# Attention products with the values on quarters of the TensorE array, attention in two PSUM rings, and a new order of the work

## The chip, the cores and the metric

The kernel runs on one core of a Trainium2 chip. The metric is the device time of one execution in microseconds (us); less is better. The engines are named as the profile names them: PE is TensorE (matmuls; PEld is its weight load), DVE is VectorE, ACT is ScalarE, POOL is GpSimd, SP is the engine that issues the DMAs. Each engine works through its own queue in the order in which the program lists it.

## What is computed

Attention with a window of 128 positions over 4 x 8 heads (576 positions, 64 wide), then a two-layer MLP over the 2304 tokens, then an expert layer for tokens with a positive skip score. The kernel counts the tokens with a positive score and leaves the expert layer out where there are none, as in the execution profiled here.

```python
scores = scale * np.matmul(q, k.transpose(0, 1, 3, 2))
mask = (rel >= 0) & (rel < window)                   # window = 128
scores = np.where(mask, scores + bias[None], -1000000000.0)
attn = np.exp(scores - scores.max(-1)); attn = attn / (attn.sum(-1) + 1e-09)
x = np.matmul(attn, v)                               # then (tokens, 512)
h = x @ w_in                                         # 512 -> 2048
g = where(h >= 1, h, where(h <= -1, 0, (h + 1) ** 2 / 4))
x = g @ w_out                                        # 2048 -> 512
```

## The kernel before

The 2304 tokens are nine blocks `g` of 256 queries (two tiles of 128). `pair` (L312) is the attention of one block for two heads; there are four pairs to a block, 36 in all. `tile_ff` (L516) is one step of the MLP: 256 tokens by two of the sixteen groups of 128 hidden units, so eight steps to a block, 72 in all. Weights and activations of the MLP are split into a high and a low float32r part, and each product is three matmuls: a step has 24 matmuls of 256 columns into `h` (L528, here "first product") and 12 of 512 columns into the block's two sums (L559, "second product", six for each tile of tokens). `weight` (L463) unpacks the weights, which come in as float64, in integer operations on DVE with copies on ACT; that work lies in about the first 120 us. Blocks 0 to 2 run interleaved, so that a weight is used three times while the next is unpacked; blocks 3 to 8 follow one after the other, with the attention of a later block between their steps.

A pair goes through these stages. SP loads q and k (`qkraw`) and v (`vraw`); q is scaled on ACT or POOL (L334, L336). PE makes the scores. For blocks 0 and 1 (`whole`) two heads lie in two row halves of the array, with 256 columns each (L347). From block 2 on, 64 queries by 192 keys at a time, so that four matmuls lie on the four 64 x 64 quarters of the array (L359). DVE puts the two parts of the window together under a mask (L370 or L376, "merge"), adds the bias and takes the row maximum (L382). ACT takes the exponential of each tile and head (L388), four to a pair. DVE inverts the sums (L397, L398). The rows are normalised on ACT (L416) or POOL (L419), transposed on PE (L424) into a PSUM bank, and copied to `pts` on ACT (L293). POOL masks the copy into `ab` (L307), four selects to a pair. PE multiplies with the values (L446): for each head one matmul of 256 columns and two of 128 columns, on a 128 x 64 half of the array, the two heads side by side. The result is copied to `xT` by ACT (L293) and its low part made by DVE (L302).

PSUM has eight banks, in four rings of two: `h` for the first product, and `r0`, `r1`, `r2`. For blocks 3 to 8 all attention goes through `r0`: scores (two banks), transposed rows (two) and products with the values (one), one after another. The sums of the second product alternate between `r2` and `r1`.

The order of the instructions on every engine is worked out before the kernel is built. `Plan.order` places the pieces with costs written in the source (for instance 2 * dve(128) + 0.06 us for the merge of one head, L391), keeps for each engine a list of what can run and takes what is due first; due times come from `PLAN` (`lead`, `spread`, `d2` and others). It is five passes over all pieces, and the tile pools then add the waits. Where the plan sees PE idle in the first 40 us, L603 puts in matmuls without use ("fills").

Of the kernel before, what the change touches and what calls it, by code (L numbers as in the profile page):

```python
# [11 lines left out]
F32 = mybir.dt.float32  # L12
# [6 lines left out]
ALU = mybir.AluOpType  # L19
# [3 lines left out]
P = 128  # L23
B, H, S, D = 4, 8, 576, 64
NT = B * S
DM = H * D
# [5 lines left out]
NPAIR = H // 2  # L32
# [13 lines left out]
PLAN = dict(base=4.418, d0=10.283, d1=3.632, d3=3, d2=5.432, lag=1, lag2=9, ahead=19.774, lead=22.491, spread=2,  # L46
            margin=1.2, slack=0.049, fin=0.449, passes=5, first=3, stick=4.711, zeros=0, whole=2)

ENGINES = dict(norm="AP", wlo="DP", rebias="A", pt="A", whi="A", square="A", scale="AP")
# [48 lines left out]
class Plan:  # L98
# [139 lines left out]
dve = lambda n: n / 960.0 + 0.072  # L238
# [7 lines left out]
class Fused:  # L246
# [50 lines left out]
    def pick(self, key, **cost):  # L297
        return {e: cost[e] for e in ENGINES[key]}

# [12 lines left out]
    def pair(self, g, p, due):  # L312
# [26 lines left out]
        lq = add(self.pick("scale", A=0.4, P=0.43, D=dve2(256)), scale, [lq], use=[qk], port=True)  # L339
        s = [self.att(g, [P, 2, 4, 64]) for _ in heads]  # L340
# [20 lines left out]
        sn = self.buf("sn", 2, [P, 4, P])  # L361
# [40 lines left out]
        for odd, o in heads:  # L402
            pt = self.bank("r1", [P, 2, P]) if g < 2 else self.att(g, [P, 2, P])
# [28 lines left out]
            d = add(self.pick("norm", A=0.586, D=dve(256), P=0.67), norm, [rs], use=[sn, st], port=True)  # L432
            d = self.chain("tr", add({"T": 0.221}, transpose, [d], new=[pt, pts], use=[sn]))
            d = add(self.pick("pt", A=actp(256), D=dve(256)), lambda e, ptv=ptv, pts=pts: self.copy(e, pts.t, ptv()), [d],
# [4 lines left out]
        av = self.att(g, [P, 2, P]) if g else self.bank("r0", [P, 2, P])  # L439

        def avs(e):
            for out, k, m, more in ((slice(0, 2), j, slice(1, 3), False), (0, 0, 0, True), (1, j + 1, 3, True)):
                if g == 0 and k == 0 and more:
                    continue
                for o, ab, _ in last:
                    nc.tensor.matmul(av.t[o, out, :], v.t[:, k, o], ab.t[:, m, :], start=not more, stop=True,  # L446
                                     skip_group_check=more)

        d = add({"T": 0.92 if g else 0.71}, avs, [lv, last[0][2], last[1][2]], new=[av], use=[v, last[0][1], last[1][1]],
                mode="cols")  # L450
        new = []
        if g not in self.xT:
# [4 lines left out]
        d1 = add({"A": actp(256)}, lambda e: self.copy(e, xT.t[:, 0, p], av.t), [d], new=new, use=[av, xT])  # L457
        d2 = add({"D": dve(256)}, lambda e: self.sub(e, xT.t[:, 1, p], av.t, xT.t[:, 0, p].bitcast(F32)), [d, d1],
                 use=[av, xT], due=due)
# [145 lines left out]
    def run(self):  # L605
# [231 lines left out]
```

## Time and profile before

| | |
|---|---|
| time, median of 3 runs | 527.0 us (526.81 to 528.45) |
| profiled execution, its own time | 527.1 us |
| its span in the profile | 525.3 us |
| PE busy | 509.4 us (97%) |
| PEld busy | 429.9 us (82%) |
| DVE busy | 277.2 us (53%) |
| ACT busy | 301.4 us (57%) |
| POOL busy | 100.7 us (19%) |
| granted TensorE clock, mean | 0.995 |

The 1.8 us between span and time lie outside what the profiler records. A matmul's busy time in the profile includes its latency, so that neighbours overlap; what a group of matmuls costs PE is read from the start of the group to the start of the next one.

### The profile page before, as it was taken

The page shows a single profiled execution, that of the slowest core. Times are in us where ns is not written, and L with a number is a line of the kernel's source. Part 1 is how long each engine was busy: PE and PEld are TensorE (multiplying, and loading weights), DVE is VectorE, ACT ScalarE, POOL GpSimd, SP SyncE. Part 2 cuts the span into 40 slices and gives each one's busy share as a digit, 9 for nine tenths or more (in the row PEclk, how much of TensorE's full clock was granted, in tenths as well). Part 3 has the DMA queues.
Part 4 walks back from the last instruction along what each step waited for, and adds up shares of the span by engine and source line. Part 5 has one row for each costly group of instructions (what it writes and reads, how often), then busy time and mean ns, then how long its engine had stood idle before and what let it go on. Part 6 is the DMA issues. An engine that isn't in the chain of part 4 may idle for free.

```text
span 525.3 us, 10059 instructions
## 1 busy us (share of the span) xinstructions
PE 509.4 (97%) x3700; PEld 429.9 (82%) x3702; DVE 277.2 (53%) x844; ACT 301.4 (57%) x784; POOL 100.7 (19%) x244
## 2 busy tenths in 40 slices
PE   7999999999999999999999999999999999999994
PEld 3567898888888898889888988888888988889883
DVE  5989999998365225532555236422653265223221
ACT  6999778777477336643575237633763277433330
POOL 2673000234014200330033002400231013200000
PEclk9999999999999999999999999999999999999997
DMA  8565555553121202120212012210212020101001
GB/s 268 163 231 192 189 178 151 190 172 113 49 90 52 61 1 92 50 61 1 67 52 65 21 49 67 57 32 1 91 52 60 1 92 1 31 0 41 1 0 44
DMA packets 27141, 41.12 MB, mean 78 GB/s; under 512 B 2000, under 2 KB 15952, under 8 KB 27088
## 3 DMA queue, kind: packets, MB, share of 16 engines
q1 hardware_dynamic: 26416, 40.12, 24.2%
q8 instruction: 30, 0.49, 0.4%
q10 hardware_dynamic: 672, 0.33, 0.2%
q14 instruction: 23, 0.19, 0.1%
HBM read 35.72 MB, written 4.72 MB: 77 GB/s over the span
## 4 chain that ended last, share of the span: by engine, by line
PE 76%; DVE 11%; ACT 5%; DMA 3%; issue 2%; POOL 0%; SPq 0%; ACTq 0%; POOLq 0%; DVEq 0%
PE h L528 32%; PE r L559 32%; PE r L446 6%; PE r L359 4%; ACT sn L388 2%; PE r L424 2%; DVE stage L494 2%; DVE wtmp L499 2%; DVE r L376 2%; DMA qkraw<-in_qk 1%; DMA stage<-in_w_in 1%; DMA stage<-in_w_out 1%; DVE stage L480 1%; DVE sn L382 1%; ACT sn L416 1%
## 5 line engine op out<-in xcount | busy, mean ns | idle before, releaser
L528 PE MATMUL h<-xT,wi 128*128 128x256 f32 x1728 | 222.9, 282 | 0.6 <-POOL wi L302 0.4
L528 PEld LDWEIGHTS h<-xT,wi 128*128 128x128 f32 x1728 | 213.6, 188 | 11.7 <-issue 5.2
L559 PE MATMUL r<-wo,g 128*128 128x512 f32 x864 | 219.1, 400 | 0.0
L559 PEld LDWEIGHTS r<-wo,g 128*128 128x128 f32 x864 | 156.0, 188 | 37.7 <-issue 4.4
L550 DVE SCALAR_TENSOR_TENSOR h<-h,u 128x512 f32<-128x512 f32 x72 | 50.3, 698 | 129.3 <-ACT u L545 126.6
L540 ACT ACTIVATE u<-h,half 128x512 f32<-128x512 f32 x72 | 49.4, 686 | 111.1 <-PE h L528 110.5
L419 POOL TENSOR_SCALAR sn<-sn,st 128x128 f32<-128x128 f32 x70 | 27.1, 400 | 237.4 <-ACT u L540 175.7
L388 ACT ACTIVATE sn<-sn,st 128x128 f32<-128x128 f32 x144 | 56.1, 391 | 27.1 <-DVE st L382 27.0
L307 POOL TENSOR_SCALAR_AFFINE_SELECT ab<-pts 128x256 f32<-128x256 f32 (+1 forms) x144 | 56.5, 426 | 53.5 <-ACT pts L293 44.0
L293 ACT ACTIVATE g<-h 128x512 fp32r<-128x512 f32 x72 | 42.8, 594 | 33.1 <-DVE h L550 32.9
L302 DVE TENSOR_TENSOR g<-h,g 128x512 fp32r<-128x512 f32 x72 | 49.6, 689 | 22.2 <-ACT g L293 21.3
L545 ACT ACTIVATE u<-u 128x512 f32<-128x512 f32 x72 | 45.5, 632 | 1.4
L376 DVE COPY_PREDICATED r<-mask,r 64x128 f32<-64x128 uint8 x112 | 33.2, 296 | 15.9 <-PE r L359 12.9
L446 PE MATMUL r<-ab,vraw 128*64 128x128 f32 (+1 forms) x416 | 35.6, 315 | 3.5 <-ACT pts L293 1.7
L446 PEld LDWEIGHTS r<-ab,vraw 128*64 128x64 f32 x416 | 25.2, 136 | 14.6 <-issue 3.8
L382 DVE CUSTOM_DVE_ANT_0 sn<-r,nrel 128x128 f32<-128x128 f32 x144 | 33.3, 286 | 0.8
L574 DVE CUSTOM_DVE_ANT_0 junk<-r,wskip 128x512 f32<-128x512 f32 x18 | 12.4, 691 | 37.1 <-ACT stage L293 36.5
L388 ACT ACTIVATION_READ_ACCUMULATOR sn<-sn,st 128x1 f32 x144 | 27.0, 188 | 0.0
L416 ACT ACTIVATE sn<-sn,st 128x128 f32<-128x128 f32 x74 | 25.4, 394 | 1.7 <-DVE st L398 1.2
L424 PE MATMUL r<-ident,sn 128*128 128x128 f32 x144 | 23.7, 277 | 1.6 <-POOL sn L419 1.2
L474 ACT ACTIVATE wtmp<-stage 128x512 f32<-128x512 f32 x32 | 21.7, 679 | 5.3 <-DVE wi L302 2.2
L359 PE MATMUL r<-qkraw 64*64 64x192 f32 x448 | 24.7, 335 | 0.0
(43 smaller groups left out, 282.1 us busy)
## 6 DMA issues: line engine op xcount, KB each, us to landing
qkraw<-in_qk SPq DMA_DIRECT2D x32, 320.0 KB, 3.0
stage<-in_w_in SPq DMA_DIRECT2D x16, 512.0 KB, 3.6
stage<-in_w_out SPq DMA_DIRECT2D x16, 512.0 KB, 3.7
vraw<-in_v SPq DMA_DIRECT2D x32, 192.0 KB, 2.7
out_x<-stage SPq DMA_DIRECT2D x18, 256.0 KB, 2.0
qkraw<-in_qk SPq DMA_DIRECT2D x4, 256.0 KB, 4.2
vraw<-in_v SPq DMA_DIRECT2D x4, 128.0 KB, 4.2
nrel<-in_nrel ACTq DMA_DIRECT2D x1, 256.0 KB, 3.9
```

What stands on the lines that cost most here:

```text
L293: self.nc.scalar.activation(out=out, in_=in_, func=AF.Copy)
L302: eng.tensor_tensor(out=out, in0=in0, in1=in1, op=ALU.subtract)
L307: self.nc.gpsimd.affine_select(out=out, in_=in_, pattern=[[0, n], [sign, P]], compare_op=ALU.is_ge if causal else ALU.is_gt, fill=0.0, base=0,
L359: nc.tensor.matmul(s[odd].t[r, i, 1 - half:4 - half, :], qk.t[o, 3 + i, r], k, start=True, stop=True)
L376: nc.vector.copy_predicated(s.t[r, 1 - j:2, 1 + half, :], self.mask[r, 1 - j:2, r], s.t[r, 1 - j:2, 3 * (1 - half), :])
L388: nc.scalar.activation(out=sn.t[:, x, :], in_=sn.t[:, x, :], func=AF.Exp, scale=-1.0, bias=st.t[:, 0, x:x + 1], accum_out=st.t[:, 1, x:x + 1])
L446: nc.tensor.matmul(av.t[o, out, :], v.t[:, k, o], ab.t[:, m, :], start=not more, stop=True, skip_group_check=more)
L528: nc.tensor.matmul(h.t[:, c, :], w[:, wz, k, :], x.t[:, xz, k].rearrange("p a b -> p (a b)"), start=k == 0 and i == 0, stop=k == NKC - 1 a ...
L540: r = add({"A": 0.167 + 0.213 * n}, lambda e: nc.scalar.activation(out=uv(), in_=hv(), func=AF.Relu, scale=0.5, bias=self.half), [d], new= ...
L545: nc.scalar.activation(out=uv(), in_=uv(), func=AF.Square)
L550: r = add({"D": dve(256 * n)}, lambda e: nc.vector.scalar_tensor_tensor(out=hv(), in0=hv(), scalar=1.0, in1=uv(), op0=ALU.max, op1=ALU.min ...
L559: nc.tensor.matmul(acc[i].t, gt.t[:, gz, c, i * P:(i + 1) * P], self.wo[:, f, wz, :], start=f == 0 and j == 0, stop=f == NF - 1 and j == 2)
```

## The change

`pair` gets a second way for the products with the values (`quarters`), used for blocks 3 to 8. It splits the keys into halves of 64: each half of the keys multiplies only with the queries that see them, and for each of two heads the two halves lie on two row halves of the array. The matmuls have 192, 64 and 128 columns in one row half and 192, 128 and 64 in the other, 12 to a pair in place of six. The row halves cannot add into one PSUM bank at a time, so there are two sums (`av[0]`, `av[1]`); ACT copies the second to SBUF (`half`, in the ring of `pts`) and DVE adds it to the first in PSUM. What follows takes the first as before.

From block 4 on (`turn`) odd pairs use ring `r2` and even pairs `r0`; the sums of the second product for blocks 3 to 8 use `r1` alone. `qkraw` has four buffers, `vraw` and `sn` three, in place of two. Block 2 gets whole scores too (`whole` 3). For blocks 3 to 8 normalising and scaling are on POOL alone and the copy to `pts` is on ACT or DVE. The low parts of the weights are all made on DVE, and the first pair of weights is unpacked with one operation more on POOL and one less on DVE (`zeros` 1). The plan's other numbers are new, and with the pairs' due times (`p | 1`: pairs come in twos) the order is worked out anew.

```diff
-            margin=1.2, slack=0.049, fin=0.449, passes=5, first=3, stick=4.711, zeros=0, whole=2)
-ENGINES = dict(norm="AP", wlo="DP", rebias="A", pt="A", whi="A", square="A", scale="AP")
+            margin=1.2, slack=0.014, fin=0.158, passes=5, first=3, stick=6, zeros=1, whole=3, turn=4, quad=3)
+ENGINES = dict(norm="P", wlo="D", rebias="A", pt="AD", whi="A", square="A", scale="P", norm0="AP", pt0="A",
+               scale0="AP")
...
-    def att(self, g, shape):
-        return self.bank("r2" if g < 3 else "r0", shape)
+    def att(self, g, p, shape):
+        return self.bank("r2" if g < 3 or g >= PLAN["turn"] and p % 2 else "r0", shape)
 
     def sums(self, g):
-        return [self.bank(("r0", "r1", "r2")[g] if g < 3 else ("r2", "r1")[g % 2], [P, DM]) for _ in range(2)]
+        return [self.bank(("r0", "r1", "r2")[g] if g < 3 else "r1", [P, DM]) for _ in range(2)]
...
-    def pick(self, key, **cost):
+    def pick(self, key, g=9, **cost):
+        if g < 3:
+            key += "0"
         return {e: cost[e] for e in ENGINES[key]}
...
-        qk = self.buf("qkraw", 2, [P, 5, P])
-        v = self.buf("vraw", 2, [P, 3, P])
+        qk = self.buf("qkraw", 4, [P, 5, P])
+        v = self.buf("vraw", 3, [P, 3, P])
...
-        sn = self.buf("sn", 2, [P, 4, P])
+        sn = self.buf("sn", 3, [P, 4, P])
...
-        av = self.att(g, [P, 2, P]) if g else self.bank("r0", [P, 2, P])
+        quad = g >= PLAN["quad"]
+        av = [self.att(g, p, [P, 2 * P]) for _ in range(2)] if quad else [
+            self.att(g, p, [P, 2, P]) if g else self.bank("r0", [P, 2, P])]
...
+        def quarters(e):
+
+
+            for n in range(3):
+                for r, parts in ((slice(0, 64), ((0, 192, j, P), (0, 64, 0, 0), (P, 256, 2, 2 * P))),
+                                 (slice(64, P), ((64, 256, j, P), (0, P, 0, 0), (192, 256, 2, 2 * P)))):
+                    a0, a1, k, x = parts[n]
+                    for o, ab, _ in last:
+                        nc.tensor.matmul(av[r.start // 64].t[o, a0:a1], v.t[r, k, o],
+                                         ab.t[r].rearrange("p m q -> p (m q)")[:, x + a0:x + a1], start=n == 0, stop=True,
+                                         skip_group_check=n > 0)
...
+        if quad:
+            half = self.buf("pts", 2, [P, 2 * P])
+            d = add({"A": actp(256)}, lambda e: self.copy(e, half.t, av[1].t), [d], new=[half], use=[av[1]])
+            d = add({"D": dve(256)}, lambda e: nc.vector.tensor_tensor(out=av[0].t, in0=av[0].t, in1=half.t, op=ALU.add), [d],
+                    use=[av[0], half])
...
-                self.pair(g, p, tau[pos[g, 0]] - c["lead"] - (NPAIR - 1 - p) * c["spread"] if g > 2 else 1e9)
+                self.pair(g, p, tau[pos[g, 0]] - c["lead"] - (NPAIR - 1 - (p if g < c["turn"] else p | 1)) * c["spread"]
+                          if g > 2 else 1e9)
```

The order on PE where two pairs are multiplied with the values, late in a block after block 3. A name such as `r_4645` is one PSUM buffer of a ring; a row with x4 is four matmuls in a row. Before:

```order
L528 MATMUL h<-xT,wi 128x256 x12
L446 MATMUL r_4645<-ab,vraw 64x256 x2
L446 MATMUL r_4645<-ab,vraw 64x128 x4
L446 MATMUL r_4652<-ab,vraw 64x256 x2
L446 MATMUL r_4652<-ab,vraw 64x128 x4
L528 MATMUL h<-xT,wi 128x256 x12
```

With the change (the second product is L583 there, the first L552, `quarters` L463):

```order
L583 MATMUL r_2717<-wo,g 128x512 x6
L583 MATMUL r_2776<-wo,g 128x512 x6
L463 MATMUL r_3321<-ab,vraw 64x192 x2
L463 MATMUL r_3322<-ab,vraw 64x192 x2
L463 MATMUL r_3321<-ab,vraw 64x64 x2
L463 MATMUL r_3322<-ab,vraw 64x128 x2
L463 MATMUL r_3321<-ab,vraw 64x128 x2
L463 MATMUL r_3322<-ab,vraw 64x64 x2
L463 MATMUL r_3335<-ab,vraw 64x192 x2
L463 MATMUL r_3336<-ab,vraw 64x192 x2
```

Each pair now fills two buffers, in 12 matmuls; two pairs still stand together, but behind a second product and no longer inside a first one.

The order on ACT around the scores that come in the middle of a step. `u` and `g` are the MLP step's activations, `sn,st` the exponentials, `pts` and `xT` the copies out of PSUM. Before:

```order
L540 ACTIVATE u<-h,half 128x512
L545 ACTIVATE u<-u 128x512
L388 ACTIVATE sn,st<-sn,st 128x128 x4
L293 ACTIVATE g<-h 128x512
L416 ACTIVATE sn<-sn,st 128x128 x2
L293 ACTIVATE pts<-r_4612 128x256
```

With the change:

```order
L295 ACTIVATE pts<-r_4339 128x256
L295 ACTIVATE pts<-r_4353 128x256
L295 ACTIVATE xT<-r_4338 128x256
L295 ACTIVATE xT<-r_4352 128x256
L564 ACTIVATE u<-h,half 128x512
L569 ACTIVATE u<-u 128x512
L392 ACTIVATE sn,st<-sn,st 128x128 x8
L295 ACTIVATE g<-h 128x512
```

Eight exponentials, those of two pairs, now stand between a step's square (`u<-u`) and its copy to `g`, where four stood; the two normalisations are gone from ACT, and the two copies of the second sums to `pts` are new.

## Rows read from the trace of the kernel before

**Rows 1.** Stages: us, then busy (count) PE, PEld, DVE, ACT, POOL; PEclk, DMA, GB/s.

```profile
25.00:45.00 20.00, 17.97 (x155) 12.94 (x152) 17.63 (x68) 19.09 (x65) 14.27 (x29) 1.00 0.62 198
...
353.00:408.00 55.00, 54.72 (x416) 46.91 (x415) 23.73 (x80) 29.14 (x79) 10.27 (x27) 1.00 0.17 49
```

**Rows 2.** Groups, PE, 45 to 518 us: busy, mean ns | idle before, releaser.

```profile
L446 PE MATMUL r<-ab,vraw 128*64 128x128 f32 x344 | 28.0, 311 | 1.8 <-ACT pts L293 1.7
```

**Rows 3.** Timeline, PE, one block: start us, us, instruction, count [idle before, releaser].

```profile
303.62 2.96 PE L559 MATMUL r<-wo,g 128*128 128x512 f32 x12
306.43 2.98 PE L528 MATMUL h<-xT,wi 128*128 128x256 f32 x24
309.25 2.96 PE L559 MATMUL r<-wo,g 128*128 128x512 f32 x12
312.14 0.88 PE L359 MATMUL r<-qkraw 64*64 64x192 f32 x16
...
330.07 0.88 PE L359 MATMUL r<-qkraw 64*64 64x192 f32 x16
330.88 3.07 PE L559 MATMUL r<-wo,g 128*128 128x512 f32 x12
333.79 0.60 PE L424 MATMUL r<-ident,sn 128*128 128x128 f32 x4
334.14 1.66 PE L528 MATMUL h<-xT,wi 128*128 128x256 f32 x12
336.51 1.96 PE L446 MATMUL r<-ab,vraw 128*64 128x256 f32 x24 [0.71 <-ACT pts L293]
338.40 1.69 PE L528 MATMUL h<-xT,wi 128*128 128x256 f32 x12
```

**Rows 4.** Timeline, PE, from 32 to 39 us: scores and products of single pairs.

```profile
32.24 1.13 PE L347 MATMUL r<-qkraw 64*128 64x256 f32 x8
33.31 0.61 PE L528 MATMUL h<-xT,wi 128*128 128x256 f32 x3
...
37.39 1.09 PE L446 MATMUL r<-ab,vraw 128*64 128x256 f32 x12
38.41 1.32 PE L528 MATMUL h<-xT,wi 128*128 128x256 f32 x9
```

**Rows 5.** Groups of instructions by line, whole span: busy us, mean ns of one | idle before.

```profile
L419 POOL TENSOR_SCALAR sn<-sn,st 128x128 f32<-128x128 f32 x70 | 27.1, 400 | 237.4 <-ACT u L540 175.7 <-PE r L559 36.3 <-DVE st L398 9.7
...
L416 ACT ACTIVATE sn<-sn,st 128x128 f32<-128x128 f32 x74 | 25.4, 394 | 1.7 <-DVE st L398 1.2
...
L293 ACT ACTIVATE pts<-r 128x256 f32<-128x256 f32 x72 | 23.8, 377 | 0.2 <-PE r L424 0.2
...
L302 DVE TENSOR_TENSOR xT<-r,xT 128x256 fp32r<-128x256 f32 x36 | 14.8, 420 | 16.6 <-ACT xT L293 16.6
```

**Rows 6.** Timeline, DVE and ACT, behind the scores that start at 330.07 us.

```profile
330.18 0.69 ACT L540 ACTIVATE u<-h,half 128x512 f32<-128x512 f32 x1 [0.17 <-PE h L528]
...
330.90 0.63 ACT L545 ACTIVATE u<-u 128x512 f32<-128x512 f32 x1
...
331.43 1.29 DVE L376 COPY_PREDICATED r<-mask,r 64x128 f32<-64x128 uint8 x4 [2.20 <-PE r L359]
332.74 0.29 DVE L382 CUSTOM_DVE_ANT_0 sn<-r,nrel 128x128 f32<-128x128 f32 x1
...
333.08 0.40 ACT L388 ACTIVATE sn<-sn,st 128x128 f32<-128x128 f32 x1 [1.55 <-DVE st L382]
...
333.71 0.70 DVE L550 SCALAR_TENSOR_TENSOR h<-h,u 128x512 f32<-128x512 f32 x1
...
334.64 0.57 ACT L293 ACTIVATE g<-h 128x512 fp32r<-128x512 f32 x1
...
334.77 0.42 DVE L397 TENSOR_SCALAR st<-st 128x4 f32<-128x4 f32 x1 [0.36 <-ACT sn L388]
...
335.32 0.66 DVE L302 TENSOR_TENSOR g<-h,g 128x512 fp32r<-128x512 f32 x1
```

More of the change, by code (lines that the diff above doesn't have):

```diff
@@ L38 @@
 SCRATCH = 1024
-PLAN = dict(base=4.418, d0=10.283, d1=3.632, d3=3, d2=5.432, lag=1, lag2=9, ahead=19.774, lead=22.491, spread=2,
-            margin=1.2, slack=0.049, fin=0.449, passes=5, first=3, stick=4.711, zeros=0, whole=2)
-ENGINES = dict(norm="AP", wlo="DP", rebias="A", pt="A", whi="A", square="A", scale="AP")
+PLAN = dict(base=2.305, d0=10.296, d1=5.046, d3=3, d2=5.412, lag=1, lag2=10, ahead=15, lead=51.395, spread=8.502,
+            margin=1.2, slack=0.014, fin=0.158, passes=5, first=3, stick=6, zeros=1, whole=3, turn=4, quad=3)
+ENGINES = dict(norm="P", wlo="D", rebias="A", pt="AD", whi="A", square="A", scale="P", norm0="AP", pt0="A",
+               scale0="AP")
 WARM = dict(start=2.2, end=40.0, room=0.2, each=0.3)
@@ L337, in scale @@
                                                                      scalar2=1.0, op0=ALU.mult, op1=ALU.mult)
-        lq = add(self.pick("scale", A=0.4, P=0.43, D=dve2(256)), scale, [lq], use=[qk], port=True)
-        s = [self.att(g, [P, 2, 4, 64]) for _ in heads]
+        lq = add(self.pick("scale", g, A=0.4, P=0.43, D=dve2(256)), scale, [lq], use=[qk], port=True)
+        s = [self.att(g, p, [P, 2, 4, 64]) for _ in heads]
         def scores(e):
@@ L402, in pair @@
         for odd, o in heads:
-            pt = self.bank("r1", [P, 2, P]) if g < 2 else self.att(g, [P, 2, P])
+            pt = self.bank("r1", [P, 2, P]) if g < 2 else self.att(g, p, [P, 2, P])
             pts = self.buf("pts", 2, [P, 2, P])
@@ L430, in before @@
                     self.select(ab.t[:, 0:4:2, :], pts.t, False)
-            d = add(self.pick("norm", A=0.586, D=dve(256), P=0.67), norm, [rs], use=[sn, st], port=True)
+            d = add(self.pick("norm", g, A=0.586, D=dve(256), P=0.67), norm, [rs], use=[sn, st], port=True)
             d = self.chain("tr", add({"T": 0.221}, transpose, [d], new=[pt, pts], use=[sn]))
-            d = add(self.pick("pt", A=actp(256), D=dve(256)), lambda e, ptv=ptv, pts=pts: self.copy(e, pts.t, ptv()), [d],
+            d = add(self.pick("pt", g, A=actp(256), D=dve(256)), lambda e, ptv=ptv, pts=pts: self.copy(e, pts.t, ptv()), [d],
                     use=[pt, pts])
@@ L445, in avs @@
                 for o, ab, _ in last:
-                    nc.tensor.matmul(av.t[o, out, :], v.t[:, k, o], ab.t[:, m, :], start=not more, stop=True,
+                    nc.tensor.matmul(av[0].t[o, out, :], v.t[:, k, o], ab.t[:, m, :], start=not more, stop=True,
                                      skip_group_check=more)
-        d = add({"T": 0.92 if g else 0.71}, avs, [lv, last[0][2], last[1][2]], new=[av], use=[v, last[0][1], last[1][1]],
-                mode="cols")
+        def quarters(e):
[7 more added lines that the diff above has]
+                                         skip_group_check=n > 0)
+        d = add({"T": 0.72 if quad else 0.92 if g else 0.71}, quarters if quad else avs, [lv, last[0][2], last[1][2]], new=av,
+                use=[v, last[0][1], last[1][1]], mode="cols")
+        if quad:
[3 more added lines that the diff above has]
+                    use=[av[0], half])
+        avv = lambda: av[0].t.rearrange("p (a b) -> p a b", b=P) if quad else av[0].t
         new = []
@@ L456, in pair @@
         xT = self.xT[g]
-        d1 = add({"A": actp(256)}, lambda e: self.copy(e, xT.t[:, 0, p], av.t), [d], new=new, use=[av, xT])
-        d2 = add({"D": dve(256)}, lambda e: self.sub(e, xT.t[:, 1, p], av.t, xT.t[:, 0, p].bitcast(F32)), [d, d1],
-                 use=[av, xT], due=due)
+        d1 = add({"A": actp(256)}, lambda e: self.copy(e, xT.t[:, 0, p], avv()), [d], new=new, use=[av[0], xT])
+        d2 = add({"D": dve(256)}, lambda e: self.sub(e, xT.t[:, 1, p], avv(), xT.t[:, 0, p].bitcast(F32)), [d, d1],
+                 use=[av[0], xT], due=due)
         self.xdone[g].append(d2)
```

## The prediction

> **What bounds the kernel now.** I read the stages first, then PE's idle time, then PE's timeline inside one block. In a block of the later part PE is busy 54.72 of 55 us, while DVE is busy 23.73 and ACT 29.14 [rows 1]. From 45 to 518 us the only sizeable idle time ahead of a PE group is the 1.8 us before the products with the values [rows 2]. So from 45 us on the time is PE's stream of work, and an edit counts by what it takes from that stream or by the holes it makes in it. The start is different: from 25 to 45 us ACT is busy 19.09 of 20 us, DVE 17.63, and PE's 17.97 hold fills too [rows 1]; there ACT and DVE set the pace. The granted clock is 1.00, the upper level of 2.4 GHz, in both stages, and nothing in the change gives PE a long pause; no term is made for it.
>
> **The products.** A group costs PE what lies between its start and the next group's. Two pairs of products together take 338.40 - 336.51 = 1.89 us [rows 3], one pair 38.41 - 37.39 = 1.02 [rows 4]. The second pair adds 0.87 us, so 0.15 belongs to the group and not to the columns. The head's half of the array streams 256 + 128 + 128 = 512 columns in 0.87 us, 1.70 ns a column. The scores test that rate on quarters: 330.88 - 330.07 = 0.81 [rows 3], less 0.15 is 0.66 us for 2 x 192 = 384 columns on each quarter, 1.72 ns a column. The new products put 192 + 64 + 128 = 384 columns on each quarter too, so 0.65 us a pair if short pieces stream as well as long ones. No row has a piece of 64 columns. If it took as long as one of 128, a quarter would stand for 448 columns, 0.76 us. I take 0.70, between the two, since the scores, nearest in form, show no loss but only at 192 columns. 24 pairs x (0.87 - 0.70) = **4.1 us gained** (2.6 to 5.3).
>
> **Fewer changes of form.** A group on part of the array also slows its neighbours: the second product ahead of scores takes 312.14 - 309.25 = 2.89, behind them 333.79 - 330.88 = 2.91, otherwise 306.43 - 303.62 = 2.81 [rows 3]. With the 0.15 that is 0.33 us a group. For blocks 3 to 8 the order has 24 groups of scores and 12 of products before, 15 and 16 now, since pairs come in twos: 5 x 0.33 = **1.7 gained**. Against it, block 2 gets whole scores: 33.31 - 32.24 = 1.07 [rows 4] for 0.81, 4 x 0.26 = **1.0 lost** on PE (DVE's merges there get shorter). The transposes stand in 46 groups, before in 39; at 0.1 an edge, as behind scores, that is 0.5 to 0.7: **0.5 lost**.
>
> **What is added to the other engines.** Each of 24 pairs adds a copy on ACT (0.38) and an addition on DVE (0.42, as the low part of `xT`) [rows 5]; 48 heads normalise on POOL at 2 x 0.40 instead of partly on ACT. ACT and DVE have 26 and 31 us free in a block [rows 1], so the work itself costs nothing. The longer chain behind the products (copy, addition, copy to `xT`, low part, twice) must end before the next scores, which take the same banks. These come a first product of 2.82 us [rows 3] after the products; counting 0.5 us from PE to ACT the two pairs' chain ends 0.9 us before that. Cover gone, it would cost what exceeds 0.9.
>
> **The new holes.** This is the term that decides. Where the scores of two pairs come between a first and a second product (four times in the last five blocks), ACT's queue now holds eight exponentials ahead of the copy to `g`, and that second-next product needs this `g`. I lay it out from the start of the scores, with durations of rows 6 and the scores at 330.07 [rows 3]. Merges begin at +1.36 (331.43) and take 1.31 a pair, so to 3.98. The first exponential starts 0.34 after the first row maximum (333.08 against 332.74): 4.32. Four take 1.56 (334.64 - 333.08), eight 3.12: 7.44. Then `g`, 0.57: 8.01. DVE's part of `h`, behind eight row maxima in DVE's queue, is done by 6.6 and not late. The inversion of the second pair's sums starts at 7.57 and takes 0.55 (335.32 - 334.77), and the low part of `g` another 0.66: 8.78. PE meanwhile needs 0.81 + 0.66 for the scores, 2.91 for the second product at hand, 2.82 for the next first product: 7.19. It waits 0.82 for `g`, works off two of six matmuls (0.47) and waits 0.30 for the low part. That is 1.1 us each time; before, with four exponentials and transposes between, the same place had slack. Where two pairs' scores come after a step's second product (three times), the exponentials end at 7.44 too, and the step's own chain of 0.72 + 0.63 + 0.70 + 0.57 us [rows 6] ends at 10.1; PE is there at 1.47 + 2.92 + 2.81 + 2.82 = 10.0, waits 0.1, and then 0.3 for the low part: 0.4. Sum 4 x 1.1 + 3 x 0.4 = **5.6 lost**. In the stretch where blocks 3 and 4 overlap, ten pairs of scores and products stand in 14 steps where eight and six stood; I found two places where the low part of `g` queues behind merges for about 1 us, and take **2.5 lost** (0 to 5). The old **1.8** [rows 2] go: that wait was for ACT's copies behind normalisations, which are off ACT now, and these transposes have a whole second product (2.81) ahead of the next products.
>
> **The start.** Up to the second step's activation ACT's queue holds 12 normalisations, 18 before: 6 x 0.39 = 2.4 us less [rows 5]; three more scalings stand against two weight copies and a copy to `xT` less. POOL gets what ACT loses, 6 x 0.40 = 2.4 us, and is busy 14.27 of 20 [rows 1]. On SP's queue more loads of q and k come ahead of weights. From 2.4 gained to 2.4 lost; ACT is the fuller engine, so I take **1.0 gained**. Buffers and the deeper rings of q, k and v only allow this.
>
> **The sum.** -4.1 - 1.7 + 1.0 + 0.5 + 5.6 + 2.5 - 1.8 - 1.0 = +1.0 us against the profiled execution's own 527.1 (525.3 of span and 1.8 around it), which lies 0.1 from the median of 527.0. Forecast **528.1 us**.
>
> **Rivals.** *The holes close.* If merges or exponentials of two pairs overlap better than one pair's rows show, the waits of 5.6 and 2.5 fall to at most 2: 527.1 - 4.1 - 1.7 + 1.5 - 1.8 - 1.0 + 1 = about 521, 519.5 to 525.5. For it speaks that ACT and DVE are half idle over a block; against it that each engine's queue is in order and the exponentials stand there in a row. *Emptying PSUM falls behind* (slower): the chain behind two pairs of products has 0.9 us of slack, and ACT and DVE serve the step as well. If a step's activations come first by one operation each (0.69 and 0.63), it ends some 0.5 to 1 us late, PE waits before the scores, and everything behind them moves: from that point 4 to 6 us over eight blocks' halves, 531 to 534. The Trainium skill, "TensorEngine Tiling (Array Packing)", section Performance Considerations, speaks against this change in the same way: tiling makes TensorE faster but not the emptying of PSUM. No row of before shows that wait. *Quarters gain nothing*: short pieces cost 0.87 us a pair as before; then 4.1 is missing, 532. The same page and section gives about 60 cycles of overhead for each matmul; by that alone twelve more passes would cost about 0.3 us a pair (an estimate), and the sum would be about 535. The rows do not show such a cost: 1.72 ns a column in 16 passes of scores, 1.70 in 12 of products [rows 3, 4].
>
> **How the numbers follow.** Forecast, 526 to 530.5: 0.45. Holes close: 0.31. PSUM falls behind: 0.18. Quarters gain nothing: 0.06. The range of 8 in 10 is 521 to 533. A measurement of this kernel can tell about 0.3% (1.6 us) from no change. The first case lies across that bound: 0.04 faster, 0.26 the same, 0.15 slower. With the second (0.29 faster, 0.02 same) and the other two (0.24 slower) that is faster 0.33, same 0.28, slower 0.39; since both signs hold much, the likeliest case's own range, 526 to 530.5, stands beside the whole.
>
> **What would show it.** In PE's timeline after: two pairs of products at 1.45 to 1.65 us where 1.89 stood; two pairs' scores at 1.46. Idle time before the second product, released by ACT's `g`, about 0.8 us where scores stand in the middle of a step; none there means the holes close. Idle time before scores, released by DVE's low part of `xT`, means PSUM falls behind. A first product of 24 matmuls that starts its unbroken run clearly later than 45 us means the start was worse. The forecast is wrong if PE's idle time from 45 us to the end stays under 3 us, or exceeds 13.

## The result, and the profile after

The changed kernel takes **514.6 us** (median of 4 runs, 514.36 to 515.93) where the kernel before took 526.9: a ratio of 0.978 (95% interval 0.976 to 0.980). The forecast was 528.1 with a range of 521 to 533; the time lies below the range, and below the rival that came nearest, "the holes close" (521).

Two lines of the page of after, the span and the busy time of each engine:

```profile
span 512.7 us, 10602 instructions
PE 502.6 (98%) x3957; PEld 431.0 (84%) x3960; DVE 295.2 (58%) x886; ACT 285.4 (56%) x725; POOL 124.9 (24%) x301
```

The stages that answer to [rows 1], with the same columns:

```profile
25.00:45.00 20.00, 19.80 (x150) 14.62 (x150) 18.93 (x68) 19.14 (x66) 15.66 (x30) 1.00 0.66 227
353.00:406.00 53.00, 53.00 (x464) 46.69 (x464) 26.71 (x88) 26.76 (x70) 11.62 (x32) 1.00 0.07 22
```

PE is still the bound: in the later part it is busy 53.00 of 53 us, and a block takes 2.5 us less (192 matmuls of the first product, eight steps, take 53.23 us from the 960th on where they took 55.69). What PE waited for from 45 us to the end (engine, line, what it waited for: us in total, times, longest) is one line:

```profile
PE tot L692 <- DVE sel L689: 1.7, 1, 1.7
```

That is the count of tokens at the very end. Nothing else is left, neither the 1.8 us of [rows 2] nor any of the new holes of the forecast, which had named an idle time under 3 us as a sign that it was wrong. One block on PE, beside [rows 3]:

```profile
300.52 3.05 PE L583 MATMUL r<-wo,g 128*128 128x512 f32 x12
303.50 1.55 PE L463 MATMUL r<-ab,vraw 64*64 64x192 f32 x48
304.98 3.09 PE L552 MATMUL h<-xT,wi 128*128 128x256 f32 x24
...
316.42 1.53 PE L363 MATMUL r<-qkraw 64*64 64x192 f32 x32
317.88 2.99 PE L552 MATMUL h<-xT,wi 128*128 128x256 f32 x24
```

Two pairs of products take 304.98 - 303.50 = 1.48 us (1.89 before), two pairs' scores 317.88 - 316.42 = 1.46 (twice 0.81 before).

And the place for which the forecast laid out the new hole, the scores of two pairs in the middle of a step. PE (the view ends at 355 us, inside the last row's group):

```profile
340.23 1.53 PE L363 MATMUL r<-qkraw 64*64 64x192 f32 x32
341.69 3.06 PE L583 MATMUL r<-wo,g 128*128 128x512 f32 x12
344.60 2.99 PE L552 MATMUL h<-xT,wi 128*128 128x256 f32 x24
347.42 2.97 PE L583 MATMUL r<-wo,g 128*128 128x512 f32 x12
...
350.58 2.97 PE L552 MATMUL h<-xT,wi 128*128 128x256 f32 x24
...
353.75 1.41 PE L583 MATMUL r<-wo,g 128*128 128x512 f32 x5
```

ACT and DVE in the same stretch (the first and the last of eight exponentials):

```profile
341.17 2.60 DVE L380 COPY_PREDICATED r<-mask,r 64x128 f32<-64x128 uint8 x8 [2.02 <-PE r L363]
...
344.13 0.40 ACT L392 ACTIVATE sn<-sn,st 128x128 f32<-128x128 f32 x1 [2.44 <-DVE st L386]
...
346.85 0.39 ACT L392 ACTIVATE sn<-sn,st 128x128 f32<-128x128 f32 x1
...
347.24 0.57 ACT L295 ACTIVATE g<-h 128x512 fp32r<-128x512 f32 x1
...
347.85 0.69 DVE L306 TENSOR_TENSOR g<-h,g 128x512 fp32r<-128x512 f32 x1
```

The chain on ACT is there as laid out, only 0.4 us earlier: eight exponentials from 344.13 to 347.24, then `g` to 347.81 and its low part to 348.54, which is 7.6 and 8.3 us behind the scores where the forecast had 8.01 and 8.78. But the second product that starts at 347.42 does not wait for this `g`. It belongs to an earlier step; this `g` is first read by the one at 353.75.

### Where the 12.6 us of span went

Each group on PE is given the time from its start to the next group's start, less idle time, and the groups are summed by kind over the whole trace (blocks 3 to 8 apart where the forecast did so). The products of blocks 3 to 8 went from 22.65 to 18.65 us, 4.0 less. The forecast's term was for their columns alone; these are taken from `halves_same_order` below, which has the new order and the old form (23.26 us, so 4.6), and the 0.6 us for four more groups go to the interruptions:

| part | forecast, us | measured, us |
|---|---|---|
| products with the values, blocks 3 to 8, columns | -4.1 | 23.26 to 18.65: -4.6 |
| whole scores in block 2 | +1.0 | +0.85 |
| interruptions: products' groups, scores' groups, slowed neighbours, transposes | -1.2 | +0.6 - 1.32 - 3.19 - 0.31 = -4.2 |
| new holes | +8.1 | 0 |
| old waits behind 45 us | -1.8 | -2.16 |
| start (idle to 45 us, products of blocks 0 to 2) | -1.0 | -1.41 + 1.32 = -0.1 |
| from the last matmul to the end | 0 | 5.74 to 3.39: -2.35 |
| sum | +1.0 | -12.6 |

Three terms are off: the holes (8.1), the interruptions (3.0) and the tail (2.35). The experiments below take them one by one.

### The profile page after: what moved, and what is told of

Same layout as the page of the kernel before. It is cut to its first block, busy times and chain, and to the rows that moved or that the text cites. A ratio compares the mean times of both kernels' runs of the same rounds, so it can differ in the third digit from the quotient of the medians.

```text
span 512.7 us, 10602 instructions
## 1 busy us (share of the span) xinstructions
PE 502.6 (98%) x3957; PEld 431.0 (84%) x3960; DVE 295.2 (58%) x886; ACT 285.4 (56%) x725; POOL 124.9 (24%) x301
## 4 chain that ended last, share of the span: by engine, by line
PE 94%; DMA 2%; DVE 2%; issue 1%; SPq 0%; POOL 0%; ACT 0%; POOLq 0%
PE h L552 41%; PE r L583 40%; PE r L463 4%; PE r L363 4%; PE r L428 3%; PE r L452 2%; PE r L351 1%; DMA stage<-in_w_in 1%; DMA stage<-in_w_out 1%; PE h L627 0%; SPq L328 0%; DVE sn L386 0%; DVE wtmp L523 0%; DVE stage L513 0%; DVE wi L306 0%
## 5 line engine op out<-in xcount | busy, mean ns | idle before, releaser
L552 PE MATMUL h<-xT,wi 128*128 128x256 f32 x1728 | 220.7, 281 | 0.3 <-DVE xT L306 0.2
L552 PEld LDWEIGHTS h<-xT,wi 128*128 128x128 f32 x1728 | 211.0, 188 | 9.4 <-issue 3.0
L583 PE MATMUL r<-wo,g 128*128 128x512 f32 x864 | 216.3, 398 | 0.0
L583 PEld LDWEIGHTS r<-wo,g 128*128 128x128 f32 x864 | 156.7, 188 | 35.3 <-issue 2.6
L311 POOL TENSOR_SCALAR_AFFINE_SELECT ab<-pts 128x256 f32<-128x256 f32 (+1 forms) x144 | 60.5, 451 | 81.9 <-ACT pts L295 60.8
L392 ACT ACTIVATE sn<-sn,st 128x128 f32<-128x128 f32 x144 | 56.0, 392 | 29.7 <-DVE st L386 29.6
L423 POOL TENSOR_SCALAR sn<-sn,st 128x128 f32<-128x128 f32 x124 | 47.5, 404 | 70.6 <-DVE st L402 46.0
L340 POOL TENSOR_SCALAR qkraw<-qkraw,qscale 128x256 f32<-128x256 f32 x26 | 15.5, 597 | 122.4 <-DMA qkraw<-in_qk 74.0
L295 ACT ACTIVATE pts<-r 128x256 f32<-128x256 f32 x71 | 26.1, 381 | 25.4 <-PE r L463 16.4
L380 DVE COPY_PREDICATED r<-mask,r 64x128 f32<-64x128 uint8 x96 | 28.4, 296 | 15.4 <-PE r L363 12.7
L297 DVE COPY pts<-r 128x256 f32<-128x256 f32 x25 | 9.7, 418 | 25.0 <-PE r L428 24.9
L523 DVE SCALAR_TENSOR_TENSOR wtmp<-wtmp,stage 128x512 int32<-128x512 int32 x32 | 22.7, 719 | 1.0 <-ACT wtmp L498 0.8
L428 PEld LDWEIGHTS r<-ident,sn 128*128 128x128 f32 x144 | 17.2, 141 | 5.8 <-ACT sn L420 1.3
```

Of the source, the lines that this page charges most:

```text
L295: self.nc.scalar.activation(out=out, in_=in_, func=AF.Copy)
L311: self.nc.gpsimd.affine_select(out=out, in_=in_, pattern=[[0, n], [sign, P]], compare_op=ALU.is_ge if causal else ALU.is_gt, fill=0.0, base=0,
L392: nc.scalar.activation(out=sn.t[:, x, :], in_=sn.t[:, x, :], func=AF.Exp, scale=-1.0, bias=st.t[:, 0, x:x + 1], accum_out=st.t[:, 1, x:x + 1])
L423: nc.gpsimd.tensor_scalar(out=sn.t[:, x, :], in0=sn.t[:, x, :], scalar1=st.t[:, 1, x:x + 1], scalar2=1.0, op0=ALU.mult, op1=ALU.mult)
L428: nc.tensor.transpose(ptv()[:, i, :], sn.t[:, 2 * odd + i, :], self.ident)
L552: nc.tensor.matmul(h.t[:, c, :], w[:, wz, k, :], x.t[:, xz, k].rearrange("p a b -> p (a b)"), start=k == 0 and i == 0, stop=k == NKC - 1 a ...
```

## The experiments

A table first. "Pieces" counts into how many unbroken pieces, from the 384th matmul of the first product on (131 us), the row of first and second products is cut by scores, products with the values or transposes: one piece more is one interruption more. "Stretch" is the time from that matmul to the 1728th and last of its kind; idle is PE's from 45 us to the last matmul of the second product. All counts and sums come from the traces' timelines.

| kernel | time, us | pieces | up to the stretch | stretch | idle |
|---|---|---|---|---|---|
| before | 526.7 | 61 | 130.9 | 378.1 | 2.2 |
| after | 514.6 | 53 | 131.2 | 367.6 | 0.0 |
| `halves_same_order` | 521.1 | 53 | 132.3 | 372.2 | 0.0 |
| `quarters_in_old_plan` | 522.3 | 73 | 131.1 | 375.1 | 0.4 |
| `one_ring` | 522.9 | 73 | 133.5 | 373.9 | 0.3 |
| `halves_in_rings` | 521.5 | 52 | 130.5 | 375.0 | 0.9 |
| `order_alone` | 527.9 | 72 | 132.5 | 379.8 | 0.3 |

### What the quarters are worth

**halves_same_order**: the changed kernel, every instruction in its place, with the old form of the products.

```diff
-        d = add({"T": 0.72 if quad else 0.92 if g else 0.71}, quarters if quad else avs, ..., new=av,
+        d = add({"T": 0.72 if quad else 0.92 if g else 0.71}, avs, ..., new=av,
...
-            d = add({"D": dve(256)}, ... tensor_tensor(out=av[0].t, in0=av[0].t, in1=half.t, op=ALU.add), ...
+            d = add({"D": dve(256)}, ... tensor_tensor(out=half.t, in0=av[0].t, in1=half.t, op=ALU.add), ...
```

The copy and the addition stay where they were (the copy now reads the first sum), but their result is not used.

> The changed kernel with the products with the values in their old form (six matmuls of 256 and 128 columns on halves of the array, into the first of the two sums), in the same order, with the copy and the addition still there but into a buffer that nothing reads. Theory: the quarters' gain is columns alone, 24 pairs x (0.87 - 0.66) = 5.0 us, so about 519.6 us, with PE still never idle behind 45 us. Rival, the gain is all from the order and the rings: 514.6, at most 515.5.

Measured 521.1 us (520.07 to 521.37), ratio to the kernel before 0.989 (0.988 to 0.991): 1.5 us above the theory, and far from the rival. PE, where the changed kernel had 1.48 us:

```profile
307.26 1.96 PE L452 MATMUL r<-ab,vraw 128*64 128x256 f32 x24
309.14 2.99 PE L552 MATMUL h<-xT,wi 128*128 128x256 f32 x24
```

1.88 us. In blocks 3 to 8 the products take 23.26 us, against 18.65: 4.6 of the 6.5 us are the products' columns. About 1.1 us more is lost before the stretch begins (0.45 of it in the products of blocks 0 to 2, which have the same form in both), for which I have no cause; the rest is that the medians lie further apart than the two profiled executions. There is still no idle time behind 45 us, so the holes are absent without the quarters too.

**quarters_in_old_plan**: the kernel before, with its plan, engines, rings and buffers, and the quarters alone.

```diff
-            margin=1.2, slack=0.049, ..., stick=4.711, zeros=0, whole=2)
+            margin=1.2, slack=0.049, ..., stick=4.711, zeros=0, whole=2, turn=9, quad=3)
```

> The kernel before with quarters alone: the old plan numbers, engines, buffers and rings, whole scores for blocks 0 and 1 only; the order follows from the plan with the new pieces in it. Theory: the columns' 5.0 us come off, and the waits before products stay near their 1.8 us or grow, since both sums lie in the one ring r0: 521 to 525. Rival (quarters need the two rings, because the longer chain behind the products holds up the next scores in the same two banks): no gain or a loss, 526 to 532.

Measured 522.3 us (522.07 to 522.53), ratio 0.992 (0.990 to 0.993): within the expectation, but partly by luck, since it had the waits stay and did not know of the tail. 24 groups of products stand there where 12 stood, one pair each:

```profile
336.04 0.89 PE L463 MATMUL r<-ab,vraw 64*64 64x192 f32 x24
336.86 3.06 PE L583 MATMUL r<-wo,g 128*128 128x512 f32 x12
```

One pair takes 0.82 us. With 1.48 for two, a pair's columns are 0.66 and a group costs 0.16 to itself. The 24 groups take 19.64 us, 22.65 before; first and second products take 1.75 us more between the 12 new interruptions, the waits fall by 1.8 and the tail (below) by 2.0. So in the old plan the quarters' own gain, 3.0 us, is more than half eaten by the neighbours of the groups that now stand singly, and 7.7 us of the change's gain come from elsewhere.

### Are there holes that were only just avoided?

**four_more_exps** and **eight_more_exps** lengthen the chain that the forecast feared: in blocks 4 to 8 every second, or every, exponential runs once more into a tile that nothing reads.

```diff
+                    if g > 3 and x % 2:    # eight_more_exps: if g > 3
+                        nc.scalar.activation(out=self.spare, in_=sn.t[:, x, :], func=AF.Exp, scale=-1.0,
+                                             bias=st.t[:, 0, x:x + 1])
```

> The changed kernel with every second exponential of blocks 4 to 8 done twice (the extra one into a buffer that nothing reads): 1.56 us more on ACT behind the scores of each two pairs, in the same order. Theory: a step's second product comes only after the next but one first product, so that g has a whole step more than the prediction gave it; what binds first is the PSUM bank of h for that next but one first product, with 2.0 us to spare where the scores stand in the middle of a step: 514.6 to 515.6. Rival, the prediction's reading (the next second product waits for this g, by 1.1 and 0.4 us already, hidden somewhere): at least seven places x 1.56 = 11 us more, 525 or above.

> The changed kernel with all exponentials of blocks 4 to 8 done twice: 3.1 us more on ACT behind the scores of each two pairs. Theory (h's bank binds, 2.0 us to spare in the middle of a step, 2.6 after a step's second product): about 1.1 us at each of four places and 0.5 at each of three, and something in blocks 3 and 4: 519 to 524 us, the first products waiting for DVE's low part of g. Rival (the next second product waits for g): 22 us more, 536 or above.

Four more: 518.4 us (517.73 to 518.61), above the theory and well below the rival. From 45 us on PE waits only where blocks 3 and 4 overlap:

```profile
PE r L432 <- DVE st L387: 0.5, 1, 0.5
PE r L364 <- DVE xT L307: 0.4, 1, 0.4
```

The steady blocks lose nothing (192 first-product matmuls from the 960th on take 53.23 us, 53.24 in the changed kernel); 1.3 us are lost before the stretch, 1.3 in the waits, 1.3 in scores and products that stretch. So a chain that is four exponentials of 0.39 us longer, 1.6 us, still holds nobody up there.

Eight more: 534.5 us (533.86 to 534.86). Now PE waits, and for what:

```profile
PE h L556 <- DVE g L307: 8.2, 7, 1.3
...
PE r L364 <- DVE xT L307: 1.7, 1, 1.7
```

It is the first product (line 556 there) that waits, for the bank of `h` that the low part of `g` has still to read, seven times in seven places of blocks 4 to 8. No second product waits. One of the seven:

```profile
343.34 0.60 ACT L296 ACTIVATE g<-h 128x512 fp32r<-128x512 f32 x1 [0.77 <-DVE h L578]
343.97 0.69 DVE L307 TENSOR_TENSOR g<-h,g 128x512 fp32r<-128x512 f32 x1 [0.66 <-ACT g L296]
344.81 2.97 PE L556 MATMUL h<-xT,wi 128*128 128x256 f32 x24 [1.15 <-DVE g L307]
```

The mechanism is the one the theory named; its size was mis-expected (19.9 us more, 5 to 9 expected), because the overlap of blocks 3 and 4 adds waits of its own (13.6 us of idle time behind 45 us in all), scores, transposes and products take 4.3 us more, and the start is again later. In the changed kernel the bank is free at 348.54 and wanted at 350.58 at the place shown above, a slack of 2.0 us. Where the scores stand behind a step's second product, as in the place shown last, the slack is 2.2 us (bank free at 327.27, wanted at 329.49), not the 2.6 of the expectation. Eight exponentials more are 3.1 us, which leaves 1.1 and 0.9; the seven waits measure 1.04 to 1.26.

### What the order and the second ring are worth

**one_ring**: all attention of the later blocks through `r0`. **halves_in_rings**: two rings, no quarters. **order_alone**: neither; what is left is the plan's numbers, the choice of engines, the buffers and block 2's whole scores. In each the order is worked out anew with the changed kernel's numbers. `turn=9` undoes two things at once, the second ring and the due times by twos (`p | 1`); no run has one without the other. A ring has two banks and the scores of one pair take both, so the scores of two pairs can't stand side by side in one ring.

```diff
-            ..., zeros=1, whole=3, turn=4, quad=3)
+            ..., zeros=1, whole=3, turn=9, quad=3)      # one_ring
+            ..., zeros=1, whole=3, turn=4, quad=9)      # halves_in_rings
+            ..., zeros=1, whole=3, turn=9, quad=9)      # order_alone, and in sums:
-        return [self.bank(("r0", "r1", "r2")[g] if g < 3 else "r1", [P, DM]) for _ in range(2)]
+        return [self.bank(("r0", "r1", "r2")[g] if g < 3 else ("r2", "r1")[g % 2], [P, DM]) for _ in range(2)]
```

> The changed kernel with the attention of all later pairs in one ring of PSUM buffers, as before (the turns begin at a block that does not exist); quarters, engines, buffers and the plan's numbers stay, the plan works out the order with them. In this order TensorE has 24 groups of scores and 24 of products from the 384th first product on, where the changed kernel has 15 and 16. Theory: what the second ring gives is pairs in twos, and a change of form costs 0.33 us a group or a little more, so 17 groups more cost about 6 us: 520 to 522, with hardly any idle time of PE behind 45 us. Rival: a change of form costs only the 0.15 of its own group: 517 to 518. A second rival: with one ring the chain behind the products (copy, addition, copy, low part) is not hidden, PE waits for it over 5 us in all and the time is over 525.

> The changed kernel without the quarters (halves for all blocks, no copy and no addition behind them), with the rings by turns; the plan works out a new order for it. 15 groups of scores and 17 of products stand from the 384th first product on, as many as with quarters. Theory: only the columns differ, 5.1 us as in the run that kept the order, so 519.5 to 520.5, below that run's 521.1 by what its later start cost. Rival: without the copy and the addition ACT and DVE gain 20 us in all, and the order closes up: under 518.

> The changed kernel without quarters and without the second ring for attention (the sums alternate between two rings as before): what is left of the change is the plan's numbers, the choice of engines, the deeper buffers and whole scores in block 2. 24 groups of scores and 24 of products stand from the 384th first product on, 24 and 12 before the change. Theory: time follows columns and groups: 12 groups more at 0.33 cost 4.0, the old waits of 1.8 go, the start and the tail as in the changed kernel or the kernel before: 526 to 530, no faster than before. Rival: the new order is worth most of the 7 us that the quarters do not explain: 519.5 to 522.

one_ring took 522.9 us (520.81 to 524.14), ratio 0.993 (0.990 to 0.995): just above the theory's range, and far from a chain that is not hidden (PE waits 0.2 us in one place). Pairs now stand singly:

```profile
331.39 0.89 PE L463 MATMUL r<-ab,vraw 64*64 64x192 f32 x24
332.21 1.68 PE L552 MATMUL h<-xT,wi 128*128 128x256 f32 x12
333.73 1.56 PE L583 MATMUL r<-wo,g 128*128 128x512 f32 x6
335.23 0.88 PE L363 MATMUL r<-qkraw 64*64 64x192 f32 x16
336.04 1.66 PE L583 MATMUL r<-wo,g 128*128 128x512 f32 x6
```

In the stretch scores and products together are 2.3 us longer than in the changed kernel, first and second products 4.3 us, with the same columns everywhere: 6.7 us for 20 more interruptions, **0.33 us each**. The transposes are 0.4 us shorter, so the stretch is 6.3 us longer; the rest is the start (2.3).

halves_in_rings took 521.5 us (520.54 to 524.57), ratio 0.992 (0.989 to 0.995). That is 1 to 2 us above the theory; the rival (under 518) falls: an order without the copy and the addition does not close up.

order_alone took 527.9 us (526.8 to 531.31), ratio 1.003 (1.001 to 1.005), as the theory had it. It has the short tail, so the rest of it is 3.5 us slower than before. Between it and halves_in_rings lie 20 interruptions, and 5.6 us in the same four kinds of group, 6.4 with the one pair of products (0.87) that halves_in_rings has more in its stretch: 0.32 each.

So neither the new numbers nor the engines are worth anything by themselves here. From order_alone the quarters give 5.0 us (one_ring), the rings 6.4 (halves_in_rings), and both 13.3. No other set of plan numbers was tried for the three.

**quarters_from_block_2** tries to go further, with four more pairs on quarters.

```diff
-            ..., turn=4, quad=3)
+            ..., turn=4, quad=2)
```

> The changed kernel with the quarters from block 2 on instead of block 3, the order worked out anew with them. Theory: four pairs more gain 0.87 - 0.67 = 0.2 us each, 0.8 in all, but in a stretch where ACT and DVE still have much to do (block 2 lies at 60 to 130 us), and each pair adds a copy and an addition there: 513.5 to 515.5. Rival: in that stretch the chain behind the products is what binds: over 516.

521.5 us (519.88 to 527.44), ratio 0.991 (0.988 to 0.994): the rival. PE's idle time behind 45 us is 5.0 us, for instance

```profile
PE h L552 <- DVE g L306: 1.5, 2, 1.4
PE r L583 <- ACT g L295: 1.0, 1, 1.0
PE r L428 <- DVE xT L306: 1.0, 1, 1.0
```

and in the first 45 us it is 6.7 (4.9 in the changed kernel). ACT and DVE end these waits. That the added copies and additions are what holds them up there is likely, but no run shows it. The changed kernel remains the fastest.

### The tail

The last work in the kernel before, and after the change, is the same small reduction on DVE; the page's span is counted to the last instruction of any engine. The kernel before, then the changed one:

```profile
core 0 of [0], span 525.3 us
...
519.59 0.17 DVE L669 TENSOR_REDUCE toti<-tot 1x1 int32<-1x18 f32 x1 [0.39 <-PE tot L667]
```

```profile
core 0 of [0], span 512.7 us
...
509.30 0.16 DVE L694 TENSOR_REDUCE toti<-tot 1x1 int32<-1x18 f32 x1 [0.39 <-PE tot L692]
```

525.3 - 519.76 = 5.5 us, and 512.7 - 509.46 = 3.2. Three runs shift DVE's code in the kernel before by 24 short settings:

```diff
-        nc.vector.memset(self.half, 0.5)
+        for _ in range(25):                                     # shifted_code
+            nc.vector.memset(self.half, 0.5)
...
             nc.vector.reciprocal(st.t[:, 1, :], st.t[:, 1, :])
+            if g > 2:
+                nc.vector.memset(self.spare, 0.5)               # shifted_code_late: a new 128x1 tile
+                nc.vector.memset(st.t[:, 0, 0:1], 0.5)          # shifted_code_no_tile: instead of it
```

> The kernel before with 24 more settings of one 128x1 tile on VectorE at its start, which nothing waits for: all that it shifts is VectorE's code. From the last matmul to the end of the span the kernel before takes 5.7 us and the changed one 3.4 with the same work. Theory: the difference is where VectorE's code happens to lie, so the tail falls to about 3.4 here and the time to about 524.5. Rival: the tail belongs to something else in the old order; it stays at 5.5 to 5.9 and the time at 526.5 to 528.

> The kernel before with the same 24 more settings of a 128x1 tile on VectorE, now one beside each pair's sums in blocks 3 to 8, where VectorE is half idle, instead of all at the start. PE's order is the same. Theory: the tail from VectorE's last work to the end of the span falls from 5.5 to about 3.3 us as in the run with the settings at the start, and nothing is lost at the start, so the time is 524 to 525. Rival: the tail is short only where the order or the start is another; it stays at 5.5 and the time at 526.5 to 527.5.

> The kernel before with 24 more settings on VectorE beside the pairs' sums in blocks 3 to 8 once more, this time into a column of a tile that the kernel has anyway (the row maxima, which are not read again there), so that no buffer moves. The run before it had a new tile of four bytes, and its first products took 120 ns a matmul where the kernel before has 118. Theory: tail 3.3 us from VectorE's last work, first products at 118 ns, span 523, time 524 to 525. Rival: the tail stays at 5.5, or something else takes the gain, and the time is 526.5 to 527.5.

shifted_code took 527.6 us (525.71 to 528.87). The tail fell as the theory had it (525.4 - 522.13 = 3.3), but the settings hold up the start, since PE's first fills wait for a tile that DVE sets behind them:

```profile
0.91 3.06 DVE L587 MEMSET half<- 128x1 f32 x25
...
521.97 0.16 DVE L670 TENSOR_REDUCE toti<-tot 1x1 int32<-1x18 f32 x1 [0.39 <-PE tot L668]
```

shifted_code_late took 526.9 us (526.31 to 528.0): tail 3.2 us, but PE's first products 3.2 us longer in sum. The new tile of four bytes moved the buffers behind it. shifted_code_no_tile moves no buffer: **524.1 us** (523.45 to 524.37), ratio 0.995 (0.993 to 0.996), with a span of

```profile
core 0 of [0], span 522.4 us
...
519.06 0.16 DVE L671 TENSOR_REDUCE toti<-tot 1x1 int32<-1x18 f32 x1 [0.39 <-PE tot L669]
```

and 3.2 us behind the last work. So 2.3 to 2.5 us of the result have nothing to do with what the change is about: they depend on where DVE's code lies. The traces show the place, among the last instructions of DVE, behind the branch that leaves the expert layer out (durations in ns, then the first and the last start in us). The kernel before, then the changed one:

```profile
L671 DVEq EVENT_SEMAPHORE  x1: 21/21/21, 521.0 to 521.0; - x1
L833 DVEq DRAIN  x2: 10/64/117, 524.4 to 524.8; - x2
```

```profile
L696 DVEq EVENT_SEMAPHORE  x1: 21/21/21, 510.7 to 510.7; - x1
L858 DVEq DRAIN  x2: 10/14/17, 510.8 to 512.2; - x2
```

Before, DVE stands still for 3.4 us between these two, and the end waits for it; after the change it goes on in 0.1 us. With one instruction more on DVE (four_bytes_more, next) the pause is 4.0 us and stands one instruction earlier, between the branch and the first of the two; with 24 more there is none. So it belongs to a place in DVE's code and not to an instruction. What DVE waits for there no run shows.

**four_bytes_more** tests the confusion of the run before by itself.

```diff
+        self.spare = c.tile([P, 1], F32, tag="spare", name="spare")
+        self.nc.vector.memset(self.spare, 0.5)
```

> The kernel before with nothing but a tile of 128x1 numbers more, in front of the other pools, set once at the start. It moves the buffers behind it by a few bytes. Theory: the first products read an operand that now lies otherwise and take 1.5 to 2 ns more each, 3.2 us in all, with one instruction more on VectorE the tail stays near 5.5: 529 to 530.5. Rival: the buffers' place is of no account, the slower matmuls belong to the settings between the sums: 526.5 to 527.5.

529.7 us (529.09 to 530.11), ratio 1.006 (1.004 to 1.007), as expected:

```profile
L674 DVEq COMPARE_BRANCH  x1: 72/72/72, 522.2 to 522.2; - x1
L674 DVEq EVENT_SEMAPHORE  x1: 21/21/21, 526.3 to 526.3; - x1
```

That is the pause at the end, and this the first product:

```profile
307.26 3.04 PE L531 MATMUL h<-xT,wi 128*128 128x256 f32 x24
310.13 2.97 PE L562 MATMUL r<-wo,g 128*128 128x512 f32 x12
```

2.87 us from the first product's start to the next group's, where [rows 3] have 309.25 - 306.43 = 2.82. Over the trace first products take 213.5 us, 210.4 before; second products are unchanged (207.4 and 207.5).

## Why the prediction was wrong, step by step

- **What bounds the kernel** was right. PE sets the time from 45 us on, and what the experiments moved lies in PE's columns, its interruptions, its waits and the two ends of the trace. Differences of 1 to 2 us ahead of the stretch are left without a cause.
- **The products** were right: 4.1 forecast, 4.6 measured. A pair's columns cost 0.66 to 0.68 us (0.70 taken, bounds 0.65 and 0.76), so pieces of 64 columns stream nearly as well as long ones. The Trainium skill, "TensorEngine Tiling (Array Packing)", section Performance Considerations, gives about 60 cycles for each matmul; no run here shows such a cost for the twelve passes that a pair has more (0.66 us for 384 columns on each quarter, 1.72 ns a column, as in the scores).
- **The new holes** are the step that failed: 8.1 us that did not come. I took the second product behind first product k+1 to read the `g` of step k. It reads an older one: two further steps lie between. The trace of before shows it at its end, where the second products of the last three steps stand alone:

```profile
506.24 2.98 PE L528 MATMUL h<-xT,wi 128*128 128x256 f32 x24
509.06 8.56 PE L559 MATMUL r<-wo,g 128*128 128x512 f32 x36
```

  36 matmuls behind the last first product are three steps of 12. I did not read that row. The times on ACT and DVE were within 0.5 us; who waits for them was wrong. With the reader right, the first wait to come is another, the bank of `h`, and eight_more_exps shows it.
- **The 2.5 us in blocks 3 and 4** rested on the same step and fell with it. That stretch does have the least slack: it is where four_more_exps waits first.
- **Fewer changes of form** had the right sign and was mis-sized: 1.2 net of transposes, measured 4.2. The price was nearly right (0.33 a group; one_ring and order_alone give 0.33 and 0.32 an interruption). The count was not: I netted the products' and scores' groups, 36 to 31, and charged the transposes as more groups, while the row of first and second products is broken eight times less often (61 pieces to 53), because groups now stand together. The transposes do stand in 46 groups, 39 before, and took 0.3 us less in place of 0.5 more. Of the rest, 3.1 us lie in the stretch, 0.39 for each of the eight (six matmuls of the second product that lie in it before the change alone, 1.4 us, are taken off); 0.8 us lie ahead of it and are not settled.
- **Whole scores** (+1.0, measured +0.85) were right. **The old waits** (-1.8, measured -2.2) were right in size; the reason given, normalisations that leave ACT, is not shown: in quarters_in_old_plan, where ACT still normalises, they fall to 0.4 us too. **The start** was forecast as -1.0 and came out at -0.1, inside its bounds of -2.4 and +2.4.
- **The tail** stood in no term. I had taken what lies behind the last matmul to be the same in both kernels; its work is, its time is not.

Of the rivals, "the holes close" had the outcome but not the reason: it let the waits shrink because merges and exponentials overlap better, and they gained 0.4 us. Its 521 became 514.6 by 1.5 us of waits that it still had, the interruptions and columns (about 3) and the tail (2.35), less the start (0.9). "Emptying PSUM falls behind" did not come: the chain behind two pairs of products never holds PE; in one ring, where pairs stand singly, it does not either. "Quarters gain nothing" is refuted by halves_same_order.

One part alone gave less than its share of the whole: from order_alone the quarters gave 5.0 us, the rings 6.4, both 13.3. The two together give about 2 us more than their sum, but the runs of each of the three kernels spread over 3 to 4.5 us, so this is not clear of the noise.

## What to carry to other kernels

Before a wait is priced on a pipelined loop, find out which iteration the reader belongs to; the end of the trace, where the pipeline empties, shows the lag in one row. When PE is the bound, count how often its long row of equal matmuls is broken, not how many small groups there are: here about a third of a microsecond a break, so two small groups side by side are cheaper than the same two apart, and a buffer ring that lets them stand together was worth as much here as fewer columns. And compare the two ends of the span between two kernels before a small difference is put down to the change.

## What the runs showed of the hardware

- Where DVE's code lies changes the end of the span: 3.2 us behind the last work in the changed kernel and with 24 more settings, 5.5 in the kernel before. The work there is the same; in the kernel before DVE pauses for 3.4 us between two of its last instructions, with one instruction more for 4.0 us one instruction earlier, with 24 more not at all.
- A tile of four bytes in front of the other buffers made every first product slower, 2.87 us for 24 matmuls in place of 2.82, and the kernel 3.2 us (0.6%); second products did not change. Which of the operands minds its place was not tried.
- Matmuls with 64 rows and 64 columns of weights on the four quarters, with 64 to 192 columns streamed, run at 0.66 to 0.68 us for 384 columns on each quarter, 1.72 to 1.77 ns a column, where the scores with 192 columns alone have 1.72.
- Each time the row of matmuls on the whole array is broken by scores or products with the values, which lie on parts of it, the small group and its neighbours lose 0.32 to 0.39 us (one_ring and order_alone over 20 breaks each, before against after over eight).
